# Random-feature attention and a gated layer on one core: stores queued earlier, next loads ahead of the last stores, one operand moved forward, five subtractions moved from GpSimd to VectorE

## The chip, the core and the metric

The kernel runs on one core of a Trainium2 chip. A core has five instruction queues that run side by side and wait for each other by semaphores: TensorE (PE in the profile; PEld is its weight load), VectorE (DVE), ScalarE (ACT), GpSimd (POOL) and SyncE (SP), which here only issues DMA transfers. Each queue runs its instructions in the order in which they stand. The metric is the device time of one execution in microseconds (us). The kernel before takes 1116.7 us, the median of three runs (1115.84 to 1117.3).

## What is computed

The reference, cut to what matters:

```python
q_s, k_s = q * scale, k * scale                      # 8 batches, 8 heads, 576 tokens, 64 wide; scale = 64 ** -0.25
def phi(x):                                          # omega: 128 x 64
    h = einsum('bhsd,md->bhsm', x, omega) - sum(x * x, -1) / 2
    return exp(h - max(h)) / sqrt(128)
kv  = einsum('bhsm,bhsd->bhmd', phi(k_s), v)
num = einsum('bhsm,bhmd->bhsd', phi(q_s), kv)
den = einsum('bhsm,bhm->bhs', phi(q_s), sum(phi(k_s), 2)) + 1e-6
x   = (num / den) as 4608 tokens x 512
out = (sigmoid(x @ w_gate) * (x @ w_val)) @ w_out    # 512 -> 1536 -> 512, weights drawn as float64
```

## The kernel before, in words

All products of the gated layer are made from two parts of each operand: `hi`, the value rounded to the format `fp32r` by a ScalarE copy, and `lo`, the rest, by a subtraction `x - hi` on VectorE or GpSimd. One product is then three matmuls: lo by hi, hi by lo and hi by hi. From the third pair of hidden tiles on, and in the output, a block product of two by two blocks is made from seven products instead of eight (`PRODUCT` names the operand and the weight of each of the seven; `p1`, `u2` and `u3` are the sums in between, and the blocks come out by additions on VectorE).

Four stages follow each other.

**Attention and first products (0 to about 476 us).** The generators `norms`, `keys`, `queries`, `first_weights`, `late_weights`, `chunk_loads`, `chunk_low`, `products`, `gate_out` and `value_out` are run by a planner (`Turns`), which gives each engine its order from estimated costs. `products` (line 500) makes gate and value of the first four hidden tiles for chunks of 512 tokens: an operand `xe` (four pieces a chunk) comes from a load `xr` (line 447), its high part from ScalarE (line 467), its low part from GpSimd (line 476, `chunk_low`). A chunk is eight products `gv` of twelve matmuls. `value_out` (line 531) multiplies value and gate on VectorE and stores `ye`. Near the end of the stage, at about 415 us, `early_unit` loads the first five weight units `u` of the next stage (896 KB each) and splits them: two high parts on ScalarE (line 437) of 768 and of 1024 columns; the low part of the first on VectorE, that of the second on GpSimd (both line 440).

**Gated units (about 477 to 832 us).** `second_pass` goes over six column blocks `c` of 768 tokens. In a block it makes eight units: four pairs of hidden tiles, each with a gate unit (kind 0) and a value unit (kind 1). `gated` is one unit, seven products of six matmuls (line 599), written in three pieces: products 1, 6, 5; products 2, 7; products 4, 3. The third piece of a unit (`held`) stands behind the first piece of the next unit, so the order on TensorE is 1, 6, 5, then 4, 3 of the unit before, then 2, 7. After a value unit seven GpSimd operations (line 648) combine gate and value into `ya` (four parts) and `yb` (three parts), which `put` stores into `yl` (line 655). There are two buffers for `ya` and one for `yb`. The operands of the next block are prepared by `operands` along a table: at (block, unit, place) certain sums (`combined`, line 560) and splits (`parts`: high on ScalarE, line 546, low on VectorE or GpSimd, line 549) are put between the pieces. Seven operands `xl` with their two parts lie in a ring of eight buffers.

**Output (about 832 us to the end).** `last(g)` makes one of 18 tiles of the output: six pairs `j`, each with seven products of three matmuls (line 768) into four banks `po`. `gated_values` loads a pair's values `yr`; for the first two pairs `sums` (line 709) makes four operands on VectorE; `parts_of` splits into `yh` (ScalarE, line 717) and `yl` (line 719; VectorE, for the last pair of a tile GpSimd). These use the same ring of eight buffers, two for a pair. Behind the last pair ScalarE copies product 1 (line 782) and VectorE makes the four blocks of `o` by seven additions (line 581); `o` lies in the buffer of `yb`. Two stores of 256 KB go out from ScalarE's queue (line 792). The third piece of the very last gated unit stands behind the first pair of tile 0, and with it the last `put`.

The gated stage, and tile 0 of the output, keep the order in which they are written (`pin`); tiles 1 to 17 are put in order by the framework's scheduler.

## Time and profile before

| | |
|---|---|
| runs | 1116.7 us median, 1115.84 to 1117.3 |
| profiled execution | 1120.23 us, of which the span of the profile is 1118.4 us |
| TensorE busy | 1063.2 us, 95% of the span |
| VectorE, ScalarE, GpSimd busy | 775.4, 490.6, 412.3 us (69, 44, 37%) |
| TensorE's share of the chain that ended last | 82% |
| mean granted TensorE clock | 0.987 of full |
| DMA | 228.67 MB, 204 GB/s over the span |

The profile gives for every instruction when it began, how long it ran, how long its engine sat idle before it and which event ended that idle time. "Busy" for TensorE means that a matmul was in flight. The granted clock is the share of full speed at which TensorE was allowed to run: at 0.50 a matmul takes twice as long and TensorE still reads as busy.

### The profile page before, as it was taken

The numbers are of one execution on the slowest core, as the hardware profiler recorded it, in microseconds if no ns is written. First come the engines' busy times: TensorE is split into PE (matmuls) and PEld (weight loads), VectorE is DVE, ScalarE is ACT, GpSimd is POOL, SyncE is SP. The second block draws the span as 40 slices with busy tenths as digits, with TensorE's granted clock in tenths as the row PEclk, the third lists the DMA queues.
The fourth block names the chain that finished last, engine by engine and source line by source line (L and its number), as shares of the span: only waits on it lengthen the run. The fifth ranks groups of instructions, "written<-read, shape, count | busy, mean of one in ns | idle before, by whom it ended". The sixth has DMA issues, their size and how long they took to land.

```text
span 1118.4 us, 26127 instructions
## 1 busy us (share of the span) xinstructions
PE 1063.2 (95%) x10412; PEld 984.9 (88%) x10412; DVE 775.4 (69%) x1483; ACT 490.6 (44%) x1011; POOL 412.3 (37%) x331
## 2 busy tenths in 40 slices
PE   3779999999999998999999999999997999999998
PEld 3668978788788787899999999999997999999998
DVE  4899999899898833456646564646655677777764
ACT  5587765756556434333323232323232433444332
POOL 0241523424241336026656575756542011111111
PEclk9899999999999998999999999999998999999999
DMA  8687989789685567152324233242986666666663
GB/s 307 205 261 245 303 309 374 262 273 342 217 299 207 187 208 287 47 204 86 130 99 156 100 121 133 77 147 82 335 311 220 192 197 188 198 193 192 191 194 101
DMA packets 122330, 228.67 MB, mean 204 GB/s; under 512 B 11104, under 2 KB 59488, under 8 KB 119136
## 3 DMA queue, kind: packets, MB, share of 16 engines
q1 hardware_dynamic: 116880, 217.49, 57.5%
q10 hardware_dynamic: 5328, 9.51, 2.3%
q8 instruction: 82, 1.34, 0.5%
q14 instruction: 40, 0.33, 0.1%
HBM read 147.26 MB, written 79.69 MB: 203 GB/s over the span
## 4 chain that ended last, share of the span: by engine, by line
PE 82%; DVE 8%; DMA 4%; ACT 3%; issue 2%; POOL 1%; SPq 1%; DVEq 0%; ACTq 0%; POOLq 0%
PE gw L599 28%; PE po L768 23%; PE gv L500 15%; PE ppk L857 3%; PE pkv L940 3%; PE pnq L1005 3%; PE ptq L988 3%; PE ppq L857 2%; PE pxq L1030 1%; DVE xl L549 1%; DMA yl<-yb 1%; ACT kpk L916 1%; DVE sqk L865 1%; DVE sqq L865 1%; DMA c2r<-w 1%
## 5 line engine op out<-in xcount | busy, mean ns | idle before, releaser
L599 PE MATMUL gw<-xl,u 128*128 128x384 f32 x2016 | 354.4, 337 | 3.6 <-DVE xl L549 3.6
L599 PEld LDWEIGHTS gw<-xl,u 128*128 128x128 f32 x2016 | 352.4, 188 | 5.3 <-DVE xl L549 4.9
L768 PE MATMUL po<-u,yh 128*128 128x256 f32 x1512 | 271.7, 283 | 0.0
L768 PEld LDWEIGHTS po<-u,yh 128*128 128x128 f32 x1512 | 234.5, 190 | 0.0
L768 PE MATMUL po<-u,yl 128*128 128x256 f32 x756 | 213.9, 283 | 7.3 <-DVE yl L719 7.3
L500 PE MATMUL gv<-xe,wh 128*128 128x512 f32 (+1 forms) x640 | 194.3, 382 | 4.1 <-POOL xe L476 4.1
L717 ACT ACTIVATE yh<-yr 128x896 fp32r<-128x896 f32 x108 | 102.9, 953 | 158.1 <-PE po L768 134.1
L768 PEld LDWEIGHTS po<-u,yl 128*128 128x128 f32 x756 | 144.4, 191 | 7.5 <-issue 7.5
L500 PEld LDWEIGHTS gv<-xe,wh 128*128 128x128 f32 x640 | 115.6, 191 | 27.0 <-POOL xe L476 5.7
L719 DVE TENSOR_TENSOR yl<-yr,yh 128x896 fp32r<-128x896 f32 x91 | 99.2, 1094 | 45.4 <-ACT yh L717 43.9
L500 PE MATMUL gv<-xe,wl 128*128 128x512 f32 (+1 forms) x320 | 121.2, 379 | 0.3 <-DVE denq L1016 0.3
L719 POOL TENSOR_TENSOR yl<-yr,yh 128x896 fp32r<-128x896 f32 x17 | 36.5, 2147 | 223.2 <-ACT yh L717 107.5
L581 DVE TENSOR_TENSOR u<-gw,p 128x384 f32<-128x384 f32 x96 | 53.2, 554 | 62.8 <-PE gw L599 47.6
L648 POOL TENSOR_TENSOR ya<-ya,g 128x384 f32<-128x384 f32 x48 | 55.6, 1158 | 104.1 <-issue 50.2
L607 ACT ACTIVATE g<-g 128x384 f32<-128x384 f32 x72 | 37.8, 526 | 109.6 <-DVE g L581 109.6
L476 POOL TENSOR_TENSOR xe<-xr,xe 128x512 fp32r<-128x512 f32 (+1 forms) x40 | 49.8, 1265 | 95.8 <-ACT xe L467 95.8
L916 ACT ACTIVATE kpk<-ppk,nbk 128x128 f32<-128x128 f32 x256 | 71.2, 392 | 15.9 <-DVE nbk L874 15.7
L709 DVE TENSOR_TENSOR yr<-yr 128x128 f32<-128x128 f32 x144 | 60.3, 460 | 21.6 <-DMA yr<-ye 20.1
L500 PEld LDWEIGHTS gv<-xe,wl 128*128 128x128 f32 x320 | 60.9, 190 | 10.7 <-PE gv L500 0.6
L857 PE MATMUL ppk<-om_sb,rawk 64*64 64x128 f32 x1152 | 45.6, 301 | 22.2 <-DMA rawk<-kT 8.2
L993 ACT ACTIVATE qpq<-ptq 128x512 f32<-128x512 f32 (+1 forms) x80 | 42.1, 557 | 47.5 <-PE ptq L988 47.3
L857 PEld LDWEIGHTS ppk<-om_sb,rawk 64*64 64x64 f32 x1152 | 35.6, 148 | 28.7 <-ACT kpk L916 10.1
(218 smaller groups left out, 1557.8 us busy)
## 6 DMA issues: line engine op xcount, KB each, us to landing
yr<-yl SPq DMA_DIRECT2D x72, 448.0 KB, 3.9
yl<-ya SPq DMA_DIRECT2D x24, 768.0 KB, 3.5
yl<-yb SPq DMA_DIRECT2D x24, 576.0 KB, 4.0
u<-w_parts SPq DMA_DIRECT2D x6, 1792.0 KB, 9.4
v<-va SPq DMA_DIRECT2D x32, 330.0 KB, 5.4
natk<-kn SPq DMA_DIRECT2D x36, 256.0 KB, 4.7
natq<-qn SPq DMA_DIRECT2D x36, 256.0 KB, 4.1
out<-o ACTq DMA_DIRECT2D x36, 256.0 KB, 2.4
```

The costliest lines, as they stand in the source:

```text
L476: nc.gpsimd.tensor_tensor(out=x[:, 1], in0=raw[:, k], in1=x[:, 0].bitcast(F32), op=ALU.subtract)
L500: nc.tensor.matmul(gv, lhsT=u[:, s], rhs=v, start=(m == 0), stop=(m == 3 * KC - 1))
L581: return nc.vector.tensor_tensor(out=o, in0=a, in1=b, op=ALU.add)
L599: nc.tensor.matmul(o, lhsT=u[:, k, s], rhs=v[:, kc, :], start=(first and m == 0), stop=(m == 5), skip_group_check=not first,)
L648: pin(nc.gpsimd.tensor_tensor(out=o, in0=a, in1=b, op=op))
L709: pin(nc.vector.tensor_tensor(out=raw[:, o], in0=raw[:, a], in1=raw[:, b], op=op))
L717: pin(nc.scalar.activation(out=yh, in_=x, func=AF.Copy))
L719: pin(engine.tensor_tensor(out=yl_, in0=x, in1=yh.bitcast(F32), op=ALU.subtract))
L768: nc.tensor.matmul(o, lhsT=u[:, i, :], rhs=v[:, k, :], start=(j + m == 0 and n in (1, 6, 5, 4)), stop=(j == NPAIR - 1 and m == 2), skip_gr ...
L857: nc.tensor.matmul(pp[r, h, k, :], lhsT=raw[HALVES[h], o + r.start : o + r.stop], rhs=om_sb[HALVES[h], :], start=True, stop=True,)
L916: nc.scalar.activation(out=kp[t][:, h, :], in_=pp[:, h, i, :], func=AF.Exp, bias=nb[:, h, i : i + 1],)
L993: nc.scalar.activation(out=qp, in_=pt, func=AF.Exp)
```

## The change

Six edits, all of order or place; no product, addition or store is left out.

1. `early_unit`: the low part of 1024 columns goes to VectorE too, instead of GpSimd, five times.
2. `operands`: the sum a12 - a11 stands one place earlier (behind unit 7 of the block before), and the split of operand 6 directly behind that of operand 2.
3. `second_pass`: `put` stands behind the first piece of a value unit, not behind its second.
4. `last`, tile 0: the loads of the first three pairs of tile 1 stand in front of the last `put`, and that `put` behind the second pair instead of the first.
5. `last`, all tiles: product 1 has a bank of its own, the order of products becomes 1, 6, 7, 5, 2, 3, 4, and the addition that reads product 2 stands two places later.
6. `last`, last tile: four stores of 128 KB, two from SP's queue and two from ScalarE's, in place of two of 256 KB.

```diff
-        for o, e, engine in ((slice(0, 3), "DVE", nc.vector), (slice(3, N_OPS), "POOL", nc.gpsimd)):
+        for o in (slice(0, 3), slice(3, N_OPS)):
...
-            t = yield e, t, None, "S" if e == "DVE" else None
-            engine.tensor_tensor(out=lo, in0=x, in1=hi.bitcast(F32), op=ALU.subtract)
-            use(e, t, dve(m) if e == "DVE" else pool_(m), LAG, "S" if e == "DVE" else None)
+            td = yield "DVE", t, None, "S"
+            nc.vector.tensor_tensor(out=lo, in0=x, in1=hi.bitcast(F32), op=ALU.subtract)
+            use("DVE", td, dve(m), LAG, "S")
...
-            (c - 1, 7, 2): [parts(1, a12, nc.vector), parts(5, a21, nc.gpsimd)],
-            (c, 0, 1): [combined(a12, a12, a11, ALU.subtract), parts(2, a22, nc.vector)],
-            (c, 0, 2): [parts(6, a12, nc.vector)],
+            (c - 1, 7, 2): [
+                parts(1, a12, nc.vector), parts(5, a21, nc.gpsimd), combined(a12, a12, a11, ALU.subtract),
+            ],
+            (c, 0, 1): [parts(2, a22, nc.vector), parts(6, a12, nc.vector)],
...
                     next(group)
+                    if kind:
+                        put()
                     between(c, n, 0)
...
                     held = group
-                    if kind:
-                        put()
...
-            for i, ns in enumerate(((1, 2), (6, 7), (5, 3), (4,))) for h, n in enumerate(ns)
+            for i, ns in enumerate(((1,), (6, 7), (5, 2), (3, 4))) for h, n in enumerate(ns)
...
-                raw = first["raws"][j] if g == 0 else gated_values(g, j)
+                raw = first["raws"][j] if g == 0 else ahead.pop(0) if ahead else gated_values(g, j)
...
             if j == 0 and held is not None:
                 next(held, None)
+                ahead[:] = [gated_values(1, i) for i in range(3)]
+            elif j == 1 and held is not None:
                 put()
...
-        add(o1[:, 0], at[2], p1)
         add(u3, at[7], u2)
         add(u2, at[5], u2)
         add(o2[:, 1], at[5], u3)
+        add(o1[:, 0], at[2], p1)
...
-        for o, r in ((o1, t), (o2, t + W)):
-            nc.scalar.dma_start(out=out[r : r + P, :], in_=o)
+        if g < NCW * SUB - 1:
+            for o, r in ((o1, t), (o2, t + W)):
+                nc.scalar.dma_start(out=out[r : r + P, :], in_=o)
+            return
+        for engine, o, i, r in ((nc.sync, o2, 1, t + W), (nc.scalar, o1, 0, t), (nc.scalar, o1, 1, t), (nc.sync, o2, 0, t + W)):
+            engine.dma_start(out=out[r : r + P, i * Q : (i + 1) * Q], in_=o[:, i])
```

The line numbers of the changed kernel are up to seven higher.

**First place: GpSimd and VectorE while the five units come in, at about 415 to 435 us.** Here GpSimd before (`u` is a unit's low part, `xe_2` and `xe_3` the third and fourth operand piece of the chunk that TensorE is about to read):

```order
L476 TENSOR_TENSOR xe_1_6940<-xr_6858,xe_1_6940 128x512
L440 TENSOR_TENSOR u_6909<-u_6909 128x1024
L440 TENSOR_TENSOR u_6916<-u_6916 128x1024
L476 TENSOR_TENSOR xe_2_7013<-xr_6858,xe_2_7013 128x512
L476 TENSOR_TENSOR xe_3_7021<-xr_6858,xe_3_7021 128x512
L440 TENSOR_TENSOR u_6920<-u_6920 128x1024
```

VectorE at the same place in the changed kernel:

```order
L440 TENSOR_TENSOR u_6909<-u_6909 128x768
L440 TENSOR_TENSOR u_6909<-u_6909 128x1024
L531 SCALAR_TENSOR_TENSOR ye_2_6991<-ge_2_6968,gv_2_1_6966 128x512
L440 TENSOR_TENSOR u_6916<-u_6916 128x768
L440 TENSOR_TENSOR u_6916<-u_6916 128x1024
L440 TENSOR_TENSOR u_6920<-u_6920 128x768
L440 TENSOR_TENSOR u_6920<-u_6920 128x1024
```

The five rows of 1024 columns are gone from GpSimd, whose `xe` rows now follow each other, and stand on VectorE behind the row of 768 columns of the same unit. ScalarE's order up to `xe_3` is the same in both.

**Second place: VectorE at the change from one column block to the next** (the first of five; `xr_1` is a12, `xl_2` and `xl_6` the low parts of operands 2 and 6). Before:

```order
L549 TENSOR_TENSOR xl_1_7877<-xr_1_7457,xl_1_7877 128x768
L581 TENSOR_TENSOR u_2_1_7893<-gw_0_2_1_7890,p_2_1_7892 128x384
L581 TENSOR_TENSOR ya_0_7747<-gw_1_5_0_7813,p_5_0_7815 128x3x128
L581 TENSOR_TENSOR ya_0_7747<-gw_1_5_0_7814,u_5_0_7816 128x3x128
L560 TENSOR_TENSOR xr_1_7457<-xr_1_7457,xr_0_7456 128x2x384
L549 TENSOR_TENSOR xl_2_7937<-xr_1_7457,xl_2_7937 128x768
L581 TENSOR_TENSOR u_2_1_7894<-gw_0_2_1_7890,p_2_1_7892 128x384
L581 TENSOR_TENSOR g_2_1_7886<-gw_0_2_1_7891,u_2_1_7894 128x384
L549 TENSOR_TENSOR xl_6_7956<-xr_1_7457,xl_6_7956 128x768
```

Now:

```order
L549 TENSOR_TENSOR xl_1_7877<-xr_1_7457,xl_1_7877 128x768
L560 TENSOR_TENSOR xr_1_7457<-xr_1_7457,xr_0_7456 128x2x384
L582 TENSOR_TENSOR u_2_1_7894<-gw_0_2_1_7891,p_2_1_7893 128x384
L582 TENSOR_TENSOR ya_0_7747<-gw_1_5_0_7813,p_5_0_7815 128x3x128
L582 TENSOR_TENSOR ya_0_7747<-gw_1_5_0_7814,u_5_0_7816 128x3x128
L549 TENSOR_TENSOR xl_2_7937<-xr_1_7457,xl_2_7937 128x768
L549 TENSOR_TENSOR xl_6_7940<-xr_1_7457,xl_6_7940 128x768
L582 TENSOR_TENSOR u_2_1_7895<-gw_0_2_1_7891,p_2_1_7893 128x384
L582 TENSOR_TENSOR g_2_1_7887<-gw_0_2_1_7892,u_2_1_7895 128x384
```

The sum (line 560) moved up by three rows, and `xl_6` by two; the second `u_2_1` (it is `u3`) and `g_2_1` now stand behind `xl_6`.

**Third place: SP and VectorE from the last gated units into the output.** SP before (the last four rows of `yl<-ya` and `yl<-yb` are the stores of the last two pairs, `yr_2` with x4 the loads of four pairs of tile 0, and what follows the stores are loads of tile 1):

```order
L411 DMA u_10545<-w_parts 128x3584
L704 DMA yr_2_10593<-yl 128x896 x4
L655 DMA yl<-ya_5_10348 128x3x512
L655 DMA yl<-yb_5_10349 128x3x384
L655 DMA yl<-ya_5_10480 128x3x512
L655 DMA yl<-yb_5_10481 128x3x384
L702 DMA yr_0_10806<-ye 128x2x128
L702 DMA yr_0_10806<-ye 128x128 x2
L702 DMA yr_1_10839<-ye 128x2x128
L702 DMA yr_1_10839<-ye 128x128 x2
L704 DMA yr_2_10872<-yl 128x896
L704 DMA yr_3_10899<-yl 128x896
```

Now:

```order
L411 DMA u_10545<-w_parts 128x3584
L656 DMA yl<-ya_5_10348 128x3x512
L656 DMA yl<-yb_5_10349 128x3x384
L705 DMA yr_2_10595<-yl 128x896 x4
L703 DMA yr_0_10665<-ye 128x2x128
L703 DMA yr_0_10665<-ye 128x128 x2
L703 DMA yr_1_10669<-ye 128x2x128
L703 DMA yr_1_10669<-ye 128x128 x2
L705 DMA yr_2_10673<-yl 128x896
L656 DMA yl<-ya_5_10480 128x3x512
L656 DMA yl<-yb_5_10481 128x3x384
L705 DMA yr_3_10899<-yl 128x896
```

The stores of the last pair but one moved ahead of four loads, and seven loads of tile 1 ahead of the stores of the last pair. Everywhere else in the gated stage SP's order is the same in both kernels.

VectorE there before (`yl_5` is the last split of tile 0, the `o` rows its blocks, then the sums and splits of tile 1):

```order
L719 TENSOR_TENSOR yl_5_10764<-yr_2_10593,yh_5_10763 128x896
L581 TENSOR_TENSOR u2o_10789<-po_0_10620,p1o_10788 128x256
L581 TENSOR_TENSOR u3o_10790<-po_0_10620,u2o_10789 128x256
L581 TENSOR_TENSOR o_10791<-po_0_10619,p1o_10788 128x256
L581 TENSOR_TENSOR u2o_10789<-po_0_10621,u2o_10789 128x256
L581 TENSOR_TENSOR o_10791<-po_0_10621,u3o_10790 128x256
L581 TENSOR_TENSOR o_10791<-po_0_10621,u2o_10789 128x256
L581 TENSOR_TENSOR o_10791<-po_0_10622,u3o_10790 128x256
L709 TENSOR_TENSOR yr_0_10806<-yr_0_10806 128x128 x4
L709 TENSOR_TENSOR yr_1_10839<-yr_1_10839 128x128 x4
L719 TENSOR_TENSOR yl_0_10815<-yr_0_10806,yh_0_10814 128x896
```

Now:

```order
L720 TENSOR_TENSOR yl_5_10774<-yr_2_10595,yh_5_10773 128x896
L710 TENSOR_TENSOR yr_0_10665<-yr_0_10665 128x128 x4
L710 TENSOR_TENSOR yr_1_10669<-yr_1_10669 128x128 x4
L720 TENSOR_TENSOR yl_0_10821<-yr_0_10665,yh_0_10820 128x896
L720 TENSOR_TENSOR yl_1_10850<-yr_1_10669,yh_1_10849 128x896
L720 TENSOR_TENSOR yl_2_10875<-yr_2_10673,yh_2_10874 128x896
L582 TENSOR_TENSOR u2o_10799<-po_0_10620,p1o_10798 128x256
L582 TENSOR_TENSOR u3o_10800<-po_0_10620,u2o_10799 128x256
L582 TENSOR_TENSOR u2o_10799<-po_0_10621,u2o_10799 128x256
L582 TENSOR_TENSOR o_10801<-po_0_10621,u3o_10800 128x256
```

The scheduler, seeing the loads of tile 1 earlier, put three pairs of tile 1 in front of tile 0's additions.

More of the change, by code (lines that the diff above doesn't have):

```diff
@@ L720, in parts_of @@
         return yh, yl_
-    first = {}
+    first, ahead = {}, []
     def first_values():
@@ L769, in last @@
                             o, lhsT=u[:, i, :], rhs=v[:, k, :],
-                            start=(j + m == 0 and n in (1, 6, 5, 4)), stop=(j == NPAIR - 1 and m == 2),
+                            start=(j + m == 0 and n in (1, 6, 5, 3)), stop=(j == NPAIR - 1 and m == 2),
                             skip_group_check=True,
```

## The prediction
> **What bounds the kernel now.** I read the page's busy line first, then a table of stretches (start and length, busy us of TensorE, its weight load, VectorE, ScalarE, GpSimd, then granted clock, DMA share, GB/s), then TensorE's waits.
>
> ```profile
> PE 1063.2 (95%) x10412; PEld 984.9 (88%) x10412; DVE 775.4 (69%) x1483; ACT 490.6 (44%) x1011; POOL 412.3 (37%) x331
> 400.00:450.00 50.00, 46.98 (x195) 37.86 (x194) 17.25 (x18) 19.81 (x29) 24.06 (x13) 0.93 0.68 245
> 850.00:900.00 50.00, 43.45 (x349) 43.48 (x350) 33.56 (x68) 19.64 (x22) 6.58 (x3) 0.93 0.70 208
> 950.00:1000.00 50.00, 50.00 (x422) 50.00 (x421) 37.53 (x69) 19.99 (x23) 6.97 (x4) 1.00 0.66 195
> PE gv L500 <- POOL xe L476: 4.1, 3, 2.7
> PE gw L599 <- DVE xl L549: 3.6, 5, 0.7
> ```
>
> TensorE is busy 95% of the span, and the output from 950 us on is without a hole: there the change can win nothing, and lose only if another engine falls behind. What it can win are TensorE's holes at the places where it moves something: one of 2.7 us that GpSimd's `xe` ends, five of 0.7 us that `xl` ends, and one near 850 us (part 3). The first and the last lie in the two stretches with a clock of 0.93, so a hole has to be read together with the clock behind it:
>
> ```profile
> 72.76 0.45 PE L857 MATMUL ppk<-om_sb,rawk 64*64 64x128 f32 x8 [2.23 <-DVE hq L970]
> 70.00:75.00 5.00, 2.77 (x82) 2.33 (x78) 4.93 (x12) 4.70 (x15) 1.90 (x3) 1.00 0.94 292
> 431.00:433.00 2.00, 1.65 (x3) 0.83 (x3) 0.93 (x2) 1.34 (x2) 2.00 (x2) 0.50 0.07 26
> 437.00:438.00 1.00, 1.00 (x5) 0.75 (x5) 0.00 (x0) 0.00 (x0) 1.00 (x1) 0.77 0.82 271
> 860.00:861.00 1.00, 1.00 (x8) 1.00 (x8) 0.00 (x0) 0.00 (x0) 0.00 (x0) 0.65 0.94 357
> ```
>
> A hole of 2.23 us left the clock at 1.00. The holes at 428 and 849 us were followed by half clock, until 437.46 (a mean of 0.77 in that microsecond is 0.46 us at half) and 860.70 (0.65).
>
> **Part 1: five subtractions to VectorE.** What TensorE waited for at 428 us:
>
> ```profile
> 424.88 1.80 ACT L437 ACTIVATE u<-u 128x768 fp32r<-128x768 f32 x2 [2.17 <-DMA u<-w]
> 427.05 0.62 ACT L467 ACTIVATE xe<-xr 128x512 fp32r<-128x512 f32 x1
> 428.31 0.62 ACT L467 ACTIVATE xe<-xr 128x512 fp32r<-128x512 f32 x1
> 426.75 2.39 POOL L440 TENSOR_TENSOR u<-u 128x1024 fp32r<-128x1024 f32 x1 [1.51 <-ACT u L437]
> 429.10 3.95 POOL L476 TENSOR_TENSOR xe<-xr,xe 128x512 fp32r<-128x512 f32 x2
> 442.58 2.54 POOL L476 TENSOR_TENSOR xe<-xr,xe 128x512 fp32r<-128x512 f32 x2 [1.78 <-ACT xe L467]
> 425.76 0.96 DVE L440 TENSOR_TENSOR u<-u 128x768 fp32r<-128x768 f32 x1 [2.25 <-ACT u L437]
> 428.44 1.51 DVE L440 TENSOR_TENSOR u<-u 128x768 fp32r<-128x768 f32 x1 [1.73 <-ACT u L437]
> 431.14 1.22 PE L500 MATMUL gv<-xe,wh 128*128 128x512 f32 x2 [2.70 <-POOL xe L476]
> 433.10 0.79 PE L500 MATMUL gv<-xe,wh 128*128 128x512 f32 x1 [0.31 <-POOL xe L476]
> ```
>
> The high part of the third piece was ready at 427.67, but GpSimd was at `u` until 429.14. The price was 2.70 + 0.31 us of waiting, and half of the 6.0 us of matmuls between 431.14 and 437.46, 3.0: together 6.0 us.
>
> In the change GpSimd is free at 427.67. But VectorE now has the work, and the rows show that such subtractions exclude each other: two `xe` take 2.54 us alone and 3.95 beside VectorE's rows of 768 columns; one of those takes 0.96 alone, and the one that began at 428.44, while GpSimd was at `u`, ended at 429.95, 0.81 behind GpSimd's end. So I let the two take turns, whole instructions at a time. VectorE's first 1024 columns start when ScalarE is through (426.68) and take 1.28 (an estimate, 0.96 x 1024 / 768); `xe_2` then runs 428.0 to 429.3, VectorE's next 768 columns to 430.2, `xe_3` to 431.5. TensorE stops at 428.44, waits 0.9, works 0.7 (an estimate: its three matmuls took 1.4 at half clock), waits 1.4 more: 2.3 in place of 6.0. **Saved 3.7.** Bounds: `xe` undisturbed (1.27 each, to 428.9 and 430.2) leaves 1.1, saved 4.9; half clock comes again behind the waits, saved 0.7. I take 3.7, since each piece is shorter than the 2.23 us that left the clock alone.
>
> VectorE pays 5 x 1.28 = 6.4 us. Its cover is its idle time, 33 of 50 us here; behind the five stands `ye`, which frees a bank that TensorE wants four products later. ScalarE's and SP's rows that change places there (a `ye` store behind eight loads) cost nothing by the same margin; without it, the 6.4 us would be the bound of the loss.
>
> **Part 2: operand 6 moved forward.**
>
> ```profile
> 542.68 2.26 PE L599 MATMUL gw<-xl,u 128*128 128x384 f32 x12
> 545.65 6.54 PE L599 MATMUL gw<-xl,u 128*128 128x384 f32 x36 [0.71 <-DVE xl L549]
> 534.96 2.55 POOL L549 TENSOR_TENSOR xl<-xr,xl 128x768 fp32r<-128x768 f32 x1
> 539.00 1.27 DVE L560 TENSOR_TENSOR xr<-xr,xr 128x768 f32<-128x768 f32 x1
> 540.18 1.77 DVE L549 TENSOR_TENSOR xl<-xr,xl 128x768 fp32r<-128x768 f32 x1
> 541.88 0.54 DVE L581 TENSOR_TENSOR u<-gw,p 128x384 f32<-128x384 f32 x1
> 544.47 1.13 DVE L549 TENSOR_TENSOR xl<-xr,xl 128x768 fp32r<-128x768 f32 x1 [1.39 <-ACT xl L546]
> ```
>
> The rows are VectorE's second place in the order: sum, `xl_2`, `u3`, and `xl_6` last. TensorE stopped at 544.94 in product 3, whose operand 6 was complete at 545.60. In the change the sum starts when GpSimd's split ends (537.5, turns again) and ends at 538.4; `u2` and the two `ya`, some 0.5 each as the row of 541.88, end at 539.9; `xl_2` and `xl_6`, 0.95 each with a GpSimd turn of 1.0 ahead of either, end at 541.5 and 543.2. That is 1.7 us before it is wanted. What is late next is `u3`: it moves from 541.88 to 543.2 and ends at 543.7, and it must have read the bank that product 4 adds to. Product 4 is the six matmuls ahead of the stop's last one, so it begins near 543.6. I leave 0.1 at each of the five block changes: **saved 5 x 0.6 = 3.0**. Bounds: 5 x 0.71 = 3.6, and 5 x 0.35 = 1.8 if `u3` is a quarter of a microsecond later.
>
> **Part 3: the crossing into the output.**
>
> ```profile
> 827.40 1.02 POOL L648 TENSOR_TENSOR yb<-ya 128x384 f32<-128x384 f32 x1
> 832.40 0.41 SPq L655 DMA_DIRECT2D yl<-yb  x1
> 841.86 1.02 POOL L648 TENSOR_TENSOR yb<-g,ya 128x384 f32<-128x384 f32 x1 [4.38 <-DMA yl<-yb]
> 837.29 4.13 DVE L719 TENSOR_TENSOR yl<-yr,yh 128x896 fp32r<-128x896 f32 x4
> 851.57 0.42 DVE L581 TENSOR_TENSOR o<-po,p1o 128x256 f32<-128x256 f32 x1 [2.37 <-DMA yl<-yb]
> 853.24 1.94 DVE L709 TENSOR_TENSOR yr<-yr 128x128 f32<-128x128 f32 x8
> 856.55 0.55 PE L768 MATMUL po<-u,yl 128*128 128x256 f32 x1 [7.29 <-DVE yl L719]
> ```
>
> `yb` of the last pair but one was complete at 828.42, but its store stood on SP behind four loads until 832.40. So GpSimd waited 4.38 us for the buffer, the last store landed at 851.5, VectorE stopped at `o` (the same buffer), and tile 1's sums and splits stood behind `o`. TensorE was idle from 849.26 to 856.55 and then half as fast to 860.70: 7.3 + 2.1 = 9.4 us.
>
> In the change that store leaves at 828.4 and GpSimd can go on at 837.48. But just then VectorE makes four splits, and turns of about 1.0 each carry the splits to 844.6 (TensorE wants the last of them at 846.8, a pair of 2.5 us ahead of 849.26) and GpSimd's last five operations to 846.9, as before. So the last `yb` store gains next to nothing; the gain is in VectorE's order. The eight sums (1.94 in all, a part of them between GpSimd's last turns) end at 848.6, `yl_0` at 849.65 (a quarter of 4.13). TensorE wants it at 849.26: it waits 0.5. From there a pair costs TensorE 2.5 us (422 matmuls in 50 us, 21 a pair) and VectorE 1.03, so three splits are ahead; `o` follows at 852 and finds its buffer stored. Of the seven loads moved ahead on SP the last stands before 840, since the buffers that they take are read by 834.4, and the stores behind them are not due before 845. **Saved 8.9.** Bounds: 6.7, if two more turns and the load of pair 1 come ahead of `yl_0`; 9.4, if nothing is left. At the other 23 places where `put` moves, SP's order stays as it was: nothing.
>
> **Part 4: the last stores and the order of additions.**
>
> ```profile
> 1114.59 0.41 DVE L581 TENSOR_TENSOR o<-po,u3o 128x256 f32<-128x256 f32 x1
> 1114.70 0.82 ACTq L792 DMA_DIRECT2D out<-o  x2
> out<-o ACTq DMA_DIRECT2D x36, 256.0 KB, 2.4
> ```
>
> Five additions instead of four stand behind the bank of product 5, which is complete one product (0.36) earlier: VectorE ends at 1115.0 as before. Then 128 KB are left to go out instead of 512 KB. A store of 256 KB takes 2.4 us from issue to landing; I let the smaller rest save **0.7**, between nothing and half of it, 1.2. [...]
>
> **Sum.** 3.7 + 3.0 + 8.9 + 0.7 = 16.3 us. The profiled execution took 1120.2 (the span of 1118.4 and 1.8 around it) and would take 1103.9. It lies 3.5 above the median of the runs, 1116.7, so the runs come to **1100.4**. All low bounds together save 9.2 (1107.5), all high ones 19.1 (1097.6).
>
> **Rivals.**
> - *Half clock again behind part 1.* For: 2.3 us of idling within 3.1 us. Against: each piece is shorter than 2.23. It loses 3.0: 1103.4. [...]
> - *Tile 1's sums wait for their load, or GpSimd takes more turns.* The eight sums stand ahead of `yl_0`, so each microsecond goes to TensorE. At 3 us more, with half clock behind them (2.0), 5.0 are lost: 1105.4.
> - *The change does not do what it says.* Parts 1 and 2 move a wait to the next in line (VectorE's `u`, `u3`) and give nothing: 1107.1. Against: both have their margin from rows above.
> - *Slower.* In every tile seven additions now stand together ahead of the fourth split:
>
> ```profile
> 1100.44 1.08 DVE L719 TENSOR_TENSOR yl<-yr,yh 128x896 fp32r<-128x896 f32 x1
> ```
>
> That is tile 17's, complete at 1101.5. Tile 17 takes 14.9 us (126 matmuls at 422 in 50 us) and ends a little before the addition at 1114.59, say 1113.9, so it began at 1099.0, and the split is wanted three pairs later, at 1106.5. Only if additions and split came 5 us later would TensorE wait; from there each microsecond costs 17. At 1.2 us beyond, 20.4 - 16.3 = 4.1 slower: 1120.8. VectorE's 37.53 of 50 us speak against it.
>
> **Chances.** Forecast 0.55, half clock 0.20, tile 1's sums 0.12, no effect of parts 1 and 2 0.07, slower 0.03, and 0.03 for a loss that I don't see and that cancels the gain. A measurement of this kernel tells about 0.2% (2.2 us) from no change. Faster 0.94, same 0.03, slower 0.03. The range takes in the bounds and the first two rivals: 1097 to 1108.
>
> **What would show it.** Right: no wait of over 1.5 us for `xe` near 428 us and a clock of 1.00 in 400 to 450; no `xl` among TensorE's waits; the wait for tile 1's `yl` under 1 us and 850 to 900 at full clock; `o` of tile 0 without a wait for a store. Wrong: `xl` waits left (part 2), a hole of several microseconds at tile 1 (part 3), TensorE waits in the later tiles (slower).

## The result, and the profile after

The changed kernel takes 1100.97 us (median of four runs, 1100.18 to 1101.6), the kernel before 1116.27 (1109.8 to 1117.3, four runs): a ratio of 0.9875 (95% interval 0.9837 to 0.9913; so in all brackets behind a ratio). The forecast was 1100.4. In a later session (e10 below) the changed kernel had a median of 1104.60 against 1117.43, ratio 0.9881 (0.9854 to 0.9908).

The changed kernel's profiled execution took 1101.05 us, its span is 1099.3. First the busy line of its page, the same stretches as before (start and length, busy us of TensorE, weight load, VectorE, ScalarE, GpSimd, then granted clock, DMA share, GB/s), and what is left among TensorE's waits on the lines that the change touches:

```profile
PE 1057.4 (96%) x10412; PEld 981.2 (89%) x10412; DVE 787.9 (72%) x1488; ACT 488.1 (44%) x1011; POOL 405.3 (37%) x326
400.00:450.00 50.00, 49.76 (x219) 40.61 (x217) 27.11 (x28) 22.78 (x34) 12.73 (x9) 1.00 0.69 250
450.00:477.00 27.00, 25.44 (x118) 21.53 (x118) 8.16 (x10) 5.80 (x10) 2.53 (x2) 1.00 0.15 53
850.00:900.00 50.00, 50.00 (x422) 50.00 (x422) 35.37 (x73) 20.85 (x26) 7.15 (x4) 1.00 0.70 210
PE gv L500 <- POOL xe L476: 2.8, 4, 1.0
```

Both stretches that had a clock of 0.93 now have 1.00. The waits for `xl` (five times 0.71) and for `yl` (7.29) are gone from the list. But 450 to 477, where TensorE was busy for all of its 27.00 us before, now has 1.56 us of idling: something has got worse there. (Of the four waits for `xe` in the last row, one of 1.0 us lies ahead of 400 us; the kernel before has it too.)

To see where the 19.1 us between the two spans (1118.4 - 1099.3) come from, the programs are cut at four events that both have: a gate `ge` of the first stage (the one at about 413 us, ten ahead of the last gate; the expectations below call it the fourth gate behind 400 us, though it is mostly the third), the first `gw`, the first `po`, the last addition `o`. The rows of the two kernels, before and then after: first from ScalarE's timeline (start, length; the number in brackets is idle time before it), then the rows of each tile (least, median and longest ns, first and last start):

```profile
413.29 0.60 ACT L518 ACTIVATE ge<-gv 128x512 f32<-128x512 f32 x1 [4.11 <-PE gv L500]
474.03 0.60 ACT L518 ACTIVATE ge<-gv 128x512 f32<-128x512 f32 x1 [4.84 <-PE gv L500]
L599 PE MATMUL gw<-xl,u x2016: 331/334/447, 476.5 to 836.4; 128*128 128x384 f32 x184
L768 PE MATMUL po<-u,yl x756: 277/282/553, 832.0 to 1113.1; 128*128 128x256 f32 x189
L581 DVE TENSOR_TENSOR o<-po,u3o x36: 411/414/425, 852.2 to 1114.6; 128x256 f32<-128x256 f32 x36
```

```profile
412.61 0.60 ACT L518 ACTIVATE ge<-gv 128x512 f32<-128x512 f32 x1 [4.11 <-PE gv L500]
469.69 0.60 ACT L518 ACTIVATE ge<-gv 128x512 f32<-128x512 f32 x1 [4.79 <-PE gv L500]
L600 PE MATMUL gw<-xl,u x2016: 331/335/359, 472.2 to 827.2; 128*128 128x384 f32 x184
L769 PE MATMUL po<-u,yl x756: 277/283/288, 822.8 to 1094.5; 128*128 128x256 f32 x189
L582 DVE TENSOR_TENSOR o<-po,u3o x36: 414/416/417, 842.8 to 1096.0; 128x256 f32<-128x256 f32 x36
```

| stretch | before | after | saved | forecast |
|---|---|---|---|---|
| up to the gate at 413 us (nothing changed there) | 413.29 | 412.61 | 0.7 | 0 |
| to the last gate (part 1), ten gates later | 60.74 | 57.08 | 3.7 | 3.7 |
| first `gw` to first `po` (part 2) | 355.5 | 350.6 | 4.9 | 3.0 |
| first `po` to the start of the last `o` (part 3) | 282.6 | 273.2 | 9.4 | 8.9 |
| from there to the end (part 4) | 3.8 | 3.3 | 0.5 | 0.7 |
| sum | | | 19.2 | 16.3 |

The stretch from the last gate to the first `gw` is left out; it is 2.5 us in both. The part sums say 19.2, the two medians 15.3. The experiments show about half of the reason: the profiled execution of the kernel before was a costly one of its kind in part 1, by some 2 us.

### The profile page after: what moved, and what is told of

It is laid out like the page before. It is cut to its first block, busy times and chain, and to the rows that moved or that the text cites. A ratio compares the mean times of both kernels' runs of the same rounds, so it can differ in the third digit from the quotient of the medians.

```text
span 1099.3 us, 26161 instructions
## 1 busy us (share of the span) xinstructions
PE 1057.4 (96%) x10412; PEld 981.2 (89%) x10412; DVE 787.9 (72%) x1488; ACT 488.1 (44%) x1011; POOL 405.3 (37%) x326
## 4 chain that ended last, share of the span: by engine, by line
PE 85%; DVE 5%; issue 4%; DMA 2%; ACT 2%; POOL 1%; SPq 0%; DVEq 0%; POOLq 0%; ACTq 0%
PE gw L600 32%; PE po L769 24%; PE gv L500 13%; PE ppk L864 3%; PE pkv L947 3%; PE ptq L995 3%; PE pnq L1012 3%; PE ppq L864 2%; PE pxq L1037 1%; ACT kpk L923 1%; POOL xe L476 1%; DVE sqq L872 1%; DMA xT<-xsq 1%; DVE sqk L872 1%; DMA xr<-xT 1%
## 5 line engine op out<-in xcount | busy, mean ns | idle before, releaser
L720 DVE TENSOR_TENSOR yl<-yr,yh 128x896 fp32r<-128x896 f32 x91 | 101.4, 1120 | 39.5 <-ACT yh L718 39.3
L649 POOL TENSOR_TENSOR ya<-ya,g 128x384 f32<-128x384 f32 x48 | 59.9, 1248 | 97.3 <-issue 43.8
L710 DVE TENSOR_TENSOR yr<-yr 128x128 f32<-128x128 f32 x144 | 57.0, 436 | 26.3 <-DMA yr<-ye 24.9
```

Source lines behind the costliest of these rows:

```text
L649: pin(nc.gpsimd.tensor_tensor(out=o, in0=a, in1=b, op=op))
L710: pin(nc.vector.tensor_tensor(out=raw[:, o], in0=raw[:, a], in1=raw[:, b], op=op))
L720: pin(engine.tensor_tensor(out=yl_, in0=x, in1=yh.bitcast(F32), op=ALU.subtract))
```

## The experiments

### One edit at a time (e1 to e4)

Each is the kernel before with one edit alone, so its diff is that edit's part of the diff above. Beside these four the kernel before took 1118.05 us (median of 28 runs, 1113.4 to 1121.97).

**e1, five subtractions to VectorE alone.**

```diff
-        for o, e, engine in ((slice(0, 3), "DVE", nc.vector), (slice(3, N_OPS), "POOL", nc.gpsimd)):
+        for o in (slice(0, 3), slice(3, N_OPS)):
...
```

> The kernel before with edit 1 alone (the five subtractions of 1024 columns on VectorE). Theory A (GpSimd alone made the hole at 428 us, and the half clock behind it was the hole's): no wait for xe of over 0.5 us at 428, granted clock 1.00 from 400 to 450, and TensorE's first gw at about 473 us in place of 476.66. The waits of 0.58 and 0.98 us at 450 us, which the changed kernel has and the kernel before has not, are there too, since VectorE's splits of xl now run beside xe: 1.6 us of the gain are lost again. About 3.6 us less than the kernel before in the profile. Theory B (the waits at 450 us come with another edit): none of them here, gw at 471, 5 us less. Theory C (the half clock is a matter of chance and not of the hole): clock below 1.00 somewhere in 400 to 477 although no hole of over 1 us is left.

1116.63 us, ratio 0.9991 (0.9978 to 1.0005): hardly a gain. Its profile has no half clock from 400 us to the crossing and the waits at 450 us, both as A says, so these waits come with edit 1. (The first `gw` is at 471.6 us instead of A's 473, because the gate at 413 us came 1.5 us sooner in this execution, at 411.83.) The changed kernel shows how (ScalarE's high part of the third `xe` piece and GpSimd's two low parts, TensorE's rows with a wait, then GpSimd and VectorE at 450 us):

```profile
424.62 0.62 ACT L467 ACTIVATE xe<-xr 128x512 fp32r<-128x512 f32 x1
425.32 3.30 POOL L476 TENSOR_TENSOR xe<-xr,xe 128x512 fp32r<-128x512 f32 x2 [8.99 <-ACT xe L467]
428.68 0.73 PE L500 MATMUL gv<-xe,wh 128*128 128x512 f32 x2 [0.24 <-POOL xe L476]
450.63 0.73 PE L500 MATMUL gv<-xe,wh 128*128 128x512 f32 x2 [0.58 <-POOL xe L476]
452.58 0.73 PE L500 MATMUL gv<-xe,wh 128*128 128x512 f32 x2 [0.98 <-POOL xe L476]
448.54 3.99 POOL L476 TENSOR_TENSOR xe<-xr,xe 128x512 fp32r<-128x512 f32 x2 [11.10 <-ACT xe L467]
448.48 0.96 DVE L1121 TENSOR_TENSOR s<-xl,xl 128x768 f32<-128x768 f32 x1
450.35 1.05 DVE L1127 TENSOR_TENSOR xl<-s,xl 128x768 fp32r<-128x768 f32 x1 [0.32 <-ACT xl L1124]
451.32 2.89 DVE L1127 TENSOR_TENSOR xl<-xl 128x768 fp32r<-128x768 f32 x2
```

At 428 us the wait forecast at 2.3 us came to 0.24. Most of that is not the turns of the two engines, which are there (GpSimd's two subtractions take 3.30 us instead of 2.54). It is that the third piece's high part was ready sooner: 12.6 us behind the gate at 413 us (425.24), where the forecast took it from the profile before, 14.4 us behind that gate (427.67). In the other twelve profiles it is 12.7 to 13.7, so the execution that the forecast was read from was the latest of all; with 12.6 the forecast's own turns would leave a wait of some 0.6 us (an estimate). What differs ahead of it is SP's load of the first unit: it left 2.03 us behind that gate there and 0.6 to 1.7 us in the others, held back by a store of `w_parts` as SP's waits have it (4.7 us there, 3.3 in the changed kernel), and by and large the later it left, the later the piece was ready.

But the chain that makes the first block's operands `xl` now runs earlier against TensorE's products: its sums and splits meet the last chunk's third and fourth `xe`, whose two subtractions take 3.99 us. In the kernel before the same two took 2.67. They had been ready just in time; now TensorE waits 0.58 and 0.98 us.

**e2, operand 6 alone.**

```diff
...
-            (c, 0, 1): [combined(a12, a12, a11, ALU.subtract), parts(2, a22, nc.vector)],
-            (c, 0, 2): [parts(6, a12, nc.vector)],
...
+                parts(1, a12, nc.vector), parts(5, a21, nc.gpsimd), combined(a12, a12, a11, ALU.subtract),
...
+            (c, 0, 1): [parts(2, a22, nc.vector), parts(6, a12, nc.vector)],
```

> The kernel before with edit 2 alone (operand 6 forward). From TensorE's first gw to its first po the kernel before takes 355.3 us, the changed one 350.4. Theory A (a stop costs more than its idle time, since the last matmul ahead of it does not overlap the next): 350.4 with this edit alone, 0.98 a stop, 4.9 us less. Theory B (a stop costs its idle time, 0.71, and another edit gives the rest): 351.7, 3.6 us less. Theory C (a remainder of 0.1 at each block change, as predicted): 352.3, 3.0 us less. The holes at 428 and 849 us stay as before.

1113.42 us, ratio 0.9957 (0.9941 to 0.9973). First `gw` at 474.7, first `po` at 825.3: 350.6 us, as in the changed kernel. Theory A: 4.9 us for five stops, 0.98 each, though the profile lists 0.71 of idle time. A stretch of the changed kernel without a stop shows why:

```profile
477.00:540.00 63.00, 63.00 (x363) 62.96 (x362) 45.66 (x66) 24.03 (x46) 35.95 (x29) 1.00 0.35 134
```

In flow a `gw` starts every 0.174 us (63.00 us for 363) and takes 0.334 (the row of `gw` above), so neighbours overlap by 0.16. A stop should lose this overlap too, which makes 0.87; that is worked out from these two rows, and the other 0.1 was not traced.

**e3, `put` alone.**

```diff
                     next(group)
+                    if kind:
+                        put()
                     between(c, n, 0)
...
                     held = group
-                    if kind:
-                        put()
```

> The kernel before with edit 3 alone (put behind the first piece of a value unit). SP's order changes only in the last block: the stores of the last pair but one stand ahead of the four loads of tile 0. Theory A (VectorE's order decides: the additions of tile 0 stand between the sums of tile 1 and its first splits, and wait for the buffer of yb): GpSimd's wait of 4.38 us is gone and the last yb store lands some 2 to 3 us earlier, but the additions still wait for it; the hole at tile 1 shrinks from 7.3 to 4 to 5 us and half clock may still follow: 2.5 to 5 us less. Theory B (the late store is the whole cause): no hole of over 0.5 us is left at tile 1, 9 us less.

1116.33 us, ratio 0.9985 (0.9971 to 0.9998). From the first `po` to the last `o` it takes 281.8 us, 0.8 less than before. Both theories fail, and this is the most useful of the four. SP, VectorE and TensorE at the crossing:

```profile
842.69 0.38 SPq L655 DMA_DIRECT2D yl<-yb  x1
843.17 4.55 SPq L702 DMA_DIRECT2D yr<-ye  x6
848.22 1.02 DVE L709 TENSOR_TENSOR yr<-yr 128x128 f32<-128x128 f32 x4 [7.53 <-DMA yr<-ye]
849.16 0.42 DVE L581 TENSOR_TENSOR o<-po,p1o 128x256 f32<-128x256 f32 x1
851.86 0.55 PE L768 MATMUL po<-u,yl 128*128 128x256 f32 x1 [5.81 <-DVE yl L719]
```

GpSimd no longer waits for its buffer, and the addition `o` no longer waits for a store, at all. Yet TensorE still stops for 5.8 us, because tile 1's loads stand on SP behind the last stores: they are issued from 843.17 on, and VectorE waits 7.53 us for the first. The late store, to which the prediction followed the chain back, was one of two causes with nearly the same end; with it gone the other holds the hole open.

**e4, tile 1's loads ahead of the last stores, alone.**

```diff
...
                 next(held, None)
+                ahead[:] = [gated_values(1, i) for i in range(3)]
+            elif j == 1 and held is not None:
                 put()
```

> The kernel before with edit 4 alone (loads of tile 1 ahead of the last stores, put behind the second pair; VectorE then makes the sums and the first three splits of tile 1 ahead of tile 0's additions). Theory A (VectorE's order decides): GpSimd still waits 4.4 us for the buffer of yb, and tile 0's additions still wait for the last store, some 5 us, but TensorE's hole at tile 1 is under 0.5 us and the clock from 850 to 900 is 1.00: 9.4 us less. Theory B (the late store decides): the wait comes back one split later, a hole of 3 us or more at the fourth pair of tile 1.

1106.88 us, ratio 0.9903 (0.9879 to 0.9926): the largest part of the change, and alone all that the crossing gave. From the first `po` (829.9) to the last `o` (1103.1) it takes 273.2 us, as the changed kernel does, and the clock from 850 to 900 us is 1.00. That is theory A, but for one point: the additions, behind three splits now, wait for no store. GpSimd still waits for its buffer; it costs nothing:

```profile
839.73 1.01 POOL L648 TENSOR_TENSOR yb<-g,ya 128x384 f32<-128x384 f32 x1 [4.38 <-DMA yl<-yb]
840.39 5.00 DVE L709 TENSOR_TENSOR yr<-yr 128x128 f32<-128x128 f32 x7 [1.09 <-DMA yr<-ye]
845.31 1.08 DVE L719 TENSOR_TENSOR yl<-yr,yh 128x896 fp32r<-128x896 f32 x1
849.68 0.42 DVE L581 TENSOR_TENSOR u2o<-po,p1o 128x256 f32<-128x256 f32 x1
```

The sums and the first splits of tile 1 are done before tile 0's additions can begin. In this kernel two things differ from before: the loads are early, and VectorE's order is turned. e12 parts them.

### Order against early loads (e12)

The changed kernel, with VectorE held to the order additions, sums, splits:

```diff
-                    sums(raw)
+                    sums(raw, pin if g == 1 else lambda x: x)
...
...
-        add(u2, at[6], p1)
+        pin_(add(u2, at[6], p1))
...
-        add(o2[:, 0], at[4], u3)
+        pin_(add(o2[:, 0], at[4], u3))
```

> The changed kernel with VectorE's order at the crossing turned back: tile 0's seven additions stand ahead of tile 1's sums and splits, while tile 1's loads stay ahead of the last stores and no buffer or store is late. Theory A (the early loads are what counts; with edit 3 alone VectorE waited 7.53 us for them): no hole of over 1 us at tile 1, 1101 to 1104 as the changed kernel. Theory B (VectorE's order counts by itself): the additions cannot begin before product 1 of tile 0 is copied, at about 841.4 us, and end 2.7 us later; four sums (1.0), the high part (0.95) and the first split (1.05) follow, to 847.2, while TensorE is through with tile 0 at about 841: a hole of 5 to 6 us with half clock behind it, 7 us or more lost of the 9.4, 1108 to 1111.

1109.63 us, ratio 0.9936 (0.9914 to 0.9957). Theory B: the hole is back, with everything it needs in time.

```profile
838.06 0.42 DVE L582 TENSOR_TENSOR u2o<-po,p1o 128x256 f32<-128x256 f32 x1 [4.05 <-PE po L769]
840.32 0.42 DVE L582 TENSOR_TENSOR o<-po,u3o 128x256 f32<-128x256 f32 x1 [0.84 <-DMA yl<-yb]
841.65 1.01 DVE L710 TENSOR_TENSOR yr<-yr 128x128 f32<-128x128 f32 x4
843.73 1.09 DVE L720 TENSOR_TENSOR yl<-yr,yh 128x896 fp32r<-128x896 f32 x1 [1.06 <-ACT yh L718]
844.97 0.55 PE L769 MATMUL po<-u,yl 128*128 128x256 f32 x1 [5.61 <-DVE yl L720]
840.00:850.00 10.00, 5.03 (x23) 5.06 (x24) 7.40 (x16) 3.70 (x5) 0.00 (x0) 0.67 0.50 164
```

The additions wait for product 1 of tile 0, which its last pair on TensorE completes, and begin at 838.06, when TensorE has 1.3 us of work left (844.97 - 5.61 = 839.36). What stands behind them comes too late for tile 1, and only 0.84 us of that is waiting for a store. From first `po` to last `o` it takes 281.4 us (822.1 to 1103.5), 8.2 of the 9.4 us are lost. So the crossing needs both: loads ahead of the stores (e3, where VectorE had no loaded values until 848.22, after TensorE had stopped at 846.05) and sums ahead of the additions (e12). The early store (edit 3) is not needed for it (e4).

### What part 1 is worth (e5, e9, e11)

**e5, the changed kernel without edit 1.** Its diff is that of e1, turned round.

> The changed kernel without edit 1 (five subtractions of 1024 columns on GpSimd again). The profiles with GpSimd's part as before show two shapes of the stop near 428 us: one hole of 2.70 us and 6.8 us of half clock (the kernel before), or two holes of about 1.0 us within 3.3 us and 3.4 us of half clock (the kernels with edit 2, 3 or 4 alone). Theory A (idle pieces add up within some 3.4 us, and half clock follows at about 2 us of them): one of these two shapes here, half clock from 430 on, no wait at 450 us, and 2 to 3 us more than the changed kernel in the usual case, 1103 to 1104. Theory B (the predicted 3.7 us holds for part 1): 1104.7. Theory C (the waits at 450 us eat it all): 1101, as the changed kernel.

1103.43 us, ratio to the kernel before 0.9880 (0.9856 to 0.9904). Theory A: from gate to gate 58.95 us (413.30 to 472.25), half clock from 432.5 on for one stretch of 3.4 us. The intervals do not separate it from the changed kernel; the stretch does, against six of the seven profiles with edit 1 that are listed below (e10 is the exception). Every profile in which GpSimd keeps its part, except the one of the kernel before, has this shape. TensorE's rows with a wait in e2, and its stretches:

```profile
429.79 0.74 PE L500 MATMUL gv<-xe,wh 128*128 128x512 f32 x2 [1.10 <-POOL xe L476]
431.74 1.21 PE L500 MATMUL gv<-xe,wh 128*128 128x512 f32 x2 [0.97 <-POOL xe L476]
430.00:432.00 2.00, 1.03 (x4) 0.54 (x4) 0.67 (x2) 1.04 (x2) 2.00 (x2) 0.94 0.06 24
432.00:434.00 2.00, 2.00 (x5) 1.55 (x6) 2.00 (x2) 0.96 (x2) 2.00 (x2) 0.50 0.57 165
434.00:436.00 2.00, 2.00 (x8) 1.59 (x7) 0.83 (x1) 0.58 (x1) 2.00 (x2) 0.70 0.93 292
```

Two stops of about 1 us, then half clock to 435.2. From gate to gate e2, e3, e4 and e5 take 58.72, 58.72, 58.74 and 58.95 us, the kernel before 60.74: mean 59.17. With edit 1 and the rest of its stretch as changed (e1, the changed kernel, e6, e7, e8, e10, e12) it is 57.25, 57.08, 57.32, 57.11, 57.54, 59.77 and 57.40: mean 57.64. So part 1 is worth 1.5 us in the mean (also without the kernel before and e10, the longest of either kind: 58.78 and 57.28), and 3.7 only against the profile that was shown.

**e9, the changed kernel with the last operands later.** If the waits at 450 us come from VectorE's splits beside `xe`, moving these out of the way must remove them:

```diff
                     y = a[n] if op is None else s
+                    if n == 5:
+                        t = (yield from after(x_ready[-1][-1], t)) + 4500
```

(the line is added ahead of the line shown, in `first_operands`)

> The changed kernel with the last sum and the last four splits of the first block's operands (x5, x0, x1, x2 in first_operands) asked for 4.5 us later in the plan, so that VectorE makes them behind the ye of the next product, at about 457 us, and not beside GpSimd's xe at 448.5 to 452.5. The operands are first read at 470 us. Theory A (the waits of 0.58 and 0.98 us at 450 us come from VectorE's splits beside xe): both waits gone, from the fourth gate behind 400 us to the last one 55.1 us in place of 57.1, and the kernel 2 us faster than the changed one beside it. Theory B (GpSimd's xe is late in itself, from ScalarE's xe at 447.8 on): waits of over 1 us stay, 57 us as before.

Theory A, though less than its 2 us. GpSimd's two subtractions take 2.54 us again, and one wait of 0.28 is left at 450 us:

```profile
449.49 2.54 POOL L476 TENSOR_TENSOR xe<-xr,xe 128x512 fp32r<-128x512 f32 x2 [11.10 <-ACT xe L467]
452.07 0.73 PE L500 MATMUL gv<-xe,wh 128*128 128x512 f32 x2 [0.28 <-POOL xe L476]
429.63 0.73 PE L500 MATMUL gv<-xe,wh 128*128 128x512 f32 x2 [0.82 <-POOL xe L476]
```

The wait at 428 us was 0.82 here (0.24 to 1.0 in the others), so gate to gate is 56.23 us, where A had 55.1. The median is 1100.39 us (1095.05 to 1105.46), ratio to the kernel before 0.9846 (0.9816 to 0.9877); the changed kernel beside it, e10, had 1104.60. This is the fastest version of the study; six runs each, with intervals that overlap, don't prove it faster than the changed kernel as a whole, but the row of GpSimd shows that the collision is gone.

**e11, half of the subtractions to VectorE.**

```diff
-        for o, e, engine in ((slice(0, 3), "DVE", nc.vector), (slice(3, N_OPS), "POOL", nc.gpsimd)):
+        for o, e, engine in ((slice(0, 3), "DVE", nc.vector), (slice(3, 5), "DVE", nc.vector), (slice(5, N_OPS), "POOL", nc.gpsimd)):
```

> The kernel before with edit 1 by half: of the 1024 columns of each of the five units VectorE takes 512 and GpSimd keeps 512. Theory A (half clock follows when idle pieces add up to some 2 us within 3.4 us; 1.6 us do not do it): TensorE's waits near 428 us come to about 1.0 us in place of 2.0 to 2.7, the clock stays at 1.00 from 400 to 470, and from the fourth gate to the last one it takes 57 to 58 us. Theory B (any stop of about 1 us at this place can start it): half clock of 3.4 us behind the waits, 59 us.

One run, 1118.39 us. TensorE's wait for the third and fourth piece is one of 0.99 us (at 430 us here) and the clock stays at 1.00 from 400 to 477: A, as far as one profile says it. Gate to gate 58.14 us, since the 1.56 us of waits at 450 are there too.

### The spread (e10)

The changed kernel once more, without an edit.

> The changed kernel once more, beside the others on the same chip. The attention stage in front of the change takes some 5 us more or less from one execution to the next (the fourth gate behind 400 us began between 408.0 and 413.3 us in the profiles so far, by stretches of half clock between 30 and 80 us). Theory A (that is the spread of the times): this kernel spreads as far as the kernel before does, 1096 to 1104, with a median near 1101, and from the fourth gate to the last one it takes 57.1 us again with no half clock. Theory B (the spread comes from half clock behind the holes at 428 and 849 us): it stays within 2 us.

1101.41 to 1106.31 us, median 1104.60. The spread is too wide for B, but the times lie some 3 us above what A gives, and one part of A fails: this profile has half clock behind the waits at 450 us, and takes 59.77 us from gate to gate. Its stretches, and the waits' own rows (0.59 and 0.98 us, as in the changed kernel's first profile):

```profile
451.34 0.73 PE L500 MATMUL gv<-xe,wh 128*128 128x512 f32 x2 [0.59 <-POOL xe L476]
453.28 0.81 PE L500 MATMUL gv<-xe,wh 128*128 128x512 f32 x2 [0.98 <-POOL xe L476]
454.00:456.00 2.00, 2.00 (x6) 1.54 (x5) 1.36 (x3) 1.33 (x2) 0.00 (x0) 0.50 0.00 0
456.00:458.00 2.00, 2.00 (x8) 1.59 (x7) 0.50 (x1) 0.00 (x0) 0.00 (x0) 0.70 0.00 0
```

It is the only one of eight profiles with this pair of waits (the changed kernel, e1, e6, e7, e8, e10, e11, e12) in which half clock follows. The larger part of the spread lies ahead of anything changed. The gate at 413 us began between 408.03 (e6) and 413.69 us (e11), and it goes with half clock in the attention stage. An estimate of what that costs TensorE, busy time by one minus the clock in the stretches of 10 us from 30 to 100 us, is 1.2 us in e6 and e8 (gate at 408.03 and 408.35), 2.3 in e7 (410.75), 4.8 in the changed kernel (412.61) and 6.3 in e11 (413.69); the rest fit within about 1.5 us. What starts it there was not looked into. Here one of these stretches in the changed kernel's profile and in e6:

```profile
30.00:40.00 10.00, 6.09 (x112) 5.48 (x113) 9.16 (x14) 3.93 (x8) 3.66 (x2) 0.73 0.62 215
```

```profile
30.00:40.00 10.00, 6.16 (x142) 5.37 (x144) 9.97 (x17) 5.18 (x12) 3.66 (x2) 1.00 0.67 220
```

### The banks and the tail (e6, e7, e8)

**e6, the changed kernel without edit 5.** The diff is edit 5's, turned round: product 1 shares a bank with product 2, the addition that reads product 2 comes second.

> The changed kernel without edit 5 (product 1 shares a bank with product 2 again, order 1, 2, 6, 7, 5, 3, 4, and the addition that reads product 2 comes second). Theory A (TensorE has no hole from tile 1 on in either order, and the last addition ends 1.4 us behind TensorE's last matmul in both): the same time as the changed kernel, 1101, within 0.3 us in the profile from the first po to the last addition. Theory B (the seven additions in a row cost something in each tile): 1 us or more faster than the changed kernel. Theory C (the edit is needed at the crossing, where the four additions behind product 1 would come between tile 1's splits): a hole at tile 1.

1102.07 us (1096.55 to 1104.46), ratio 0.9871 (0.9836 to 0.9905). From first `po` (818.5) to the start of the last `o` (1091.7) 273.2 us, as in the changed kernel, and no hole at tile 1: A. Edit 5 neither gains nor loses; the rival "slower" had nothing to it.

**e7 and e8, the last stores.** Four of 128 KB from one queue, and two of 256 KB from two queues:

```diff
-        for engine, o, i, r in ((nc.sync, o2, 1, t + W), (nc.scalar, o1, 0, t), (nc.scalar, o1, 1, t), (nc.sync, o2, 0, t + W)):
+        for engine, o, i, r in ((nc.scalar, o2, 1, t + W), (nc.scalar, o1, 0, t), (nc.scalar, o1, 1, t), (nc.scalar, o2, 0, t + W)):
```

> The changed kernel with the last four stores of 128 KB all issued from ScalarE's queue. From the last addition's end to the end of the span the kernel before takes 3.4 us, the changed one 2.9. Theory A (the smaller rest counts, issue is hidden behind the additions): 2.9 again. Theory B (issue time counts: an issue takes some 0.4 us, and only the last one stands behind the last addition, but the four queue up): 3.1 to 3.4.

```diff
-        for engine, o, i, r in ((nc.sync, o2, 1, t + W), (nc.scalar, o1, 0, t), (nc.scalar, o1, 1, t), (nc.sync, o2, 0, t + W)):
-            engine.dma_start(out=out[r : r + P, i * Q : (i + 1) * Q], in_=o[:, i])
+        nc.scalar.dma_start(out=out[t : t + P, :], in_=o1)
+        nc.sync.dma_start(out=out[t + W : t + W + P, :], in_=o2)
```

> The changed kernel with two last stores of 256 KB as before, one from ScalarE's queue and one from SP's. From the last addition's end to the end of the span: theory A (the size of what is left counts): 3.2 to 3.4, since 256 KB are left behind the last addition instead of 128; theory B (the second queue alone brings the gain): 2.9.

One run each, 1099.49 and 1097.80 us. From the end of the last addition to the end of the span: 3.4 us with the stores of the kernel before (itself, e1 to e4, e11: six out of six); 3.1 in e7 (1094.63 to 1097.7); 3.4 in e8 (1092.64 to 1096.0); 2.7 to 2.9 with the changed kernel's stores (itself, e5, e6, e9, e10, e12: six out of six). So e7 is at the near end of B, and e8 is A, as far as one profile of each says it: the size of the rest gives 0.3 us, a second queue alone nothing that shows, and a second queue for four stores another 0.2 to 0.4. The last issue ended 0.86 us behind the last addition in e7 and 0.36 in the changed kernel, and the second queue gained no more than these 0.5 us; whether issue time is all that it saves was not shown.

## Why the prediction was right, and where it was not

The time was right (1100.4 forecast, 1100.97 measured), and the four parts went where they were said to go. That the time came out within 0.6 us was luck in part: the stretches saved 2.9 us more than the sum (19.2 against 16.3, and 0.7 of it ahead of the change), and an offset of 3.5 us that was carried over was not there. Inside part 1 two waits were wrong in opposite directions as well, so that its 3.7 came out too.

- **The offset.** "It lies 3.5 above the median of the runs, ... so the runs come to 1100.4": this carried the excess of the profiled execution over to the changed kernel. The profiled execution of the changed kernel has none (1101.05 beside 1100.97). By the sum alone its profile would have taken 1103.9, 2.9 too much. Some 2 us of the excess were in part 1 itself: 60.74 us from gate to gate, where its like take 58.7 to 59.0, with the late load told under e1.
- **Part 1, 3.7 forecast, 3.7 against that profile, 1.5 in the mean.** Right in sign, and wrong in what was late next. The wait forecast at 428 us (2.3) came to 0.24 (0.24 to 0.97 in the eight profiles with edit 1), mainly because the start of the third piece, 427.67, was taken from an execution in which it was late (e1). Waits that were not forecast, at 450 us, came to 1.56. The step that failed is "VectorE pays 5 x 1.28 = 6.4 us. Its cover is its idle time": time was there, but I did not ask which GpSimd instruction the work that moves with it (the operands of the first block) would then meet. A row was also read a little short: the three matmuls between the two pieces took 1.65 us at half clock (431.14 to 432.79), not 1.4, and 0.98 at full clock in e2, not 0.7. And half clock was not quite half the speed, as "half of the 6.0 us" had it: in the profile before three matmuls `gv` took 1.28 us from start to start at a clock of 0.50 (434.12 to 435.40) and 0.68 at 1.00 (438.42 to 439.10), 1.9 times, and three `po` 0.64 (857.33 to 857.97) and 0.36 (861.33 to 861.69), 1.8 times. By these rows half clock cost 2.8 us there, not 3.0, and 1.8 at the crossing, not 2.1 (an estimate).
- **Part 1, the clock.** "I take 3.7, since each piece is shorter than the 2.23 us that left the clock alone" does not hold. Four profiles (e2 to e5) have two pieces of 1.0 to 1.4 us, each shorter, and half clock behind them. In e2 it was 2.1 us of idling in 3.1, with 3.4 us of half clock behind it (431.78 to 435.20); the kernel before had half clock for 6.8 us (430.62 to 437.46), from within its hole of 2.70 us on. So the length of the longest piece does not decide by itself. Had the wait come to 2.3 us in two pieces as forecast, the rival with half clock would have been the likely one (an estimate from these four profiles). What does decide was not shown: the same two waits of 0.6 and 1.0 us had 3.4 us of half clock behind them in one profile of eight (e10) and none in the other seven. The 3.4 us within which theory A of e5 and of e11 adds pieces up was not shown either: no run varied the distance, which in e2 to e5 was 3.0 to 3.3 us from the start of the first stop to the end of the second.
- **Part 2, 3.0 forecast, 4.9 measured.** The mechanism was right, the term mis-sized: a stop of 0.71 us cost 0.98 (e2), and the remainder of 0.1 at each block change, for `u3`, did not appear.
- **Part 3, 8.9 forecast, 9.4 measured.** "The gain is in VectorE's order" was right: with the order turned back 8.2 us are lost (e12). The account of the cause was incomplete: I followed the chain of waits to the late `yb` store, and e3 shows that removing it leaves 5.8 of the 7.3 us, since tile 1's loads were as late. VectorE's splits and GpSimd's last operations took turns, as forecast (an operation of GpSimd 1.86 us at 831.91 where it takes 1.02 alone, at 842.83 in the profile before; two splits 3.73 us at 830.99 where four took 4.13), and the times held within 1 us: counted from the first `po` (832.0 before, 822.8 now), the last `yb` store left at 14.0 us (14.9 before, and the forecast was "next to nothing" less), and tile 1's first split was ready at about 16.7, where the forecast had 17.7 and TensorE wanted it at 17.3. So the half microsecond left over for `yl_0` was not needed:

```profile
834.64 3.58 DVE L710 TENSOR_TENSOR yr<-yr 128x128 f32<-128x128 f32 x8
836.84 0.37 SPq L656 DMA_DIRECT2D yl<-yb  x1
838.43 3.10 DVE L720 TENSOR_TENSOR yl<-yr,yh 128x896 fp32r<-128x896 f32 x3 [0.21 <-ACT yh L718]
843.10 0.41 DVE L582 TENSOR_TENSOR o<-po,p1o 128x256 f32<-128x256 f32 x1
```

- **Part 4, 0.7 forecast, 0.5 measured**, and edit 5 at nothing, as said.
- **Alone and together.** The medians of e1 to e4 are 1.4, 4.6, 1.7 and 11.2 us below that of the kernel before beside them, 18.9 in all. That is more than the 13 to 15 that the changed kernel shows, but each median stands on a spread of several us, and e3 and e4 mend the same hole. With 1.5 for part 1 the stretches come to 16.3 us (1.5 + 4.9 + 9.4 + 0.5); why the medians show less was not traced, and the spread ahead of the change is larger than the difference.

## What to carry to other kernels

When a chain of waits ends at one late transfer, look for what else stands late in the same queue: a cause can have a twin with the same end, and only taking one away shows the other. Count a stop of TensorE as its idle time and the overlap that it breaks (0.98 us for 0.71 of idling here, e2). When you ask for the clock, look at the pieces of idling that lie close together and not at the longest alone: here two of 1.0 to 1.4 us within 3.3 had half clock behind them in four profiles of four, two of 0.6 and 1.0 in one of eight. When you take an offset from one profiled execution to the runs, ask first which part of it the change removes.

## What was not expected of the hardware

- Half clock, for 3.4 us, behind two stops of 1.0 to 1.4 us within 3.3 us (four profiles of four), behind two of 0.6 and 1.0 once in eight, and not behind a single one of 0.7 to 1.0 (e8 to e11, near 428 us).
- The attention stage, the same in every kernel, ends up to 5.7 us earlier or later from one execution to the next (408.03 to 413.69 us at the same gate), mostly with half clock between 30 and 80 us (a mean clock of 0.73 from 30 to 40 us in the changed kernel's profile, 1.00 in e6's), so single runs of one kernel differ by more than most parts of this change are worth.
- A subtraction on GpSimd beside VectorE's sums and splits takes some 2.0 us instead of 1.27 (two in 3.99 us, at 448.54), with no wait shown on either engine: the collision reads as work.
